# Squared-ReLU attention and a max-out layer on one core: the last part of z loaded by SyncE in f32, cast on ScalarE and VectorE, and transposed earlier

## The chip, the core and the metric

The kernel runs on one core of a Trainium2 chip. The core has four engines that compute here: TensorE (PE; its weight loads are shown as PEld), VectorE (DVE), ScalarE (ACT) and GpSimd (POOL). SyncE (SP) and GpSimd issue DMA transfers. Each engine executes its own instructions in order, and semaphores tie the engines together. The metric is the device time of one execution, in microseconds (us).

## The reference

Eight sequences of 3072 tokens go through an attention without softmax, and its result through a layer that takes the larger of two products.

```
u, v: (8, 3072, 256)    z: (8, 3072, 64)
scores = z @ z.T / 3072
attn = maximum(scores, 0) ** 2
x = (u * (attn @ v)).reshape(24576, 256)
h1, h2 = x @ w1, x @ w2                  # 256 to 1024
out = maximum(h1, h2) @ w_out            # 1024 to 256, f32
```

## The kernel before

**Tiling.** A sequence has 24 blocks of 128 tokens; four blocks make a group, so there are six groups per sequence and 48 steps in all, one for each (sequence b, group s). In a step TensorE forms the scores of the group against the blocks of keys, two blocks at a time (a "pair" k0, 1024 columns in one of three double banks of PSUM). ScalarE or VectorE clamps them at zero into bf16 (`relu`, L281) and squares them (`square`, L287). TensorE multiplies the squares with v into two accumulators (`acc`). The scores are symmetric, so blocks that are needed again are transposed by SyncE's DMA instead of being computed twice. The first steps multiply with v directly; later ones use sums and differences of blocks (`es`) and of v (`lf`, "folds"), which VectorE forms, to save products. Behind a step its result is multiplied by u and goes through the second layer, and SyncE stores it.

**Who orders the work.** TensorE's order is a list that is written out (`pe_order`). The orders of ScalarE, VectorE, SyncE's and GpSimd's queues come from a planner that runs while the kernel is built: `find_orders` (L1865) steps through a model of the engines with fixed durations and gives each free engine the job with the earliest due time; `find_dues` derives these times from TensorE's plan. It runs 24 rounds and the plan in which TensorE ends first is kept. The model's time zero is the start of the first planned job of TensorE. What precedes it, the head, is written out by hand, and the planner is only told when it ends: `HEAD_DONE` (L1801) says when the clamp of tile 4 is done, `idle_from` (L1866) when ScalarE and VectorE become free, in nanoseconds.

**The head** is where the change lies. z of the first sequence must reach TensorE as `zT`, transposed and in bf16:

- z's 24 blocks are loaded in three parts. SyncE loads blocks 0 to 4 and 5 to 8 (ZF = 9) as f32 into `zf`, a buffer of the pool `opool` (name o_sb, two buffers). VectorE casts the first part into `z_sb_0` (L184), ScalarE the second (L185). GpSimd loads blocks 9 to 23 in one DMA (L183) that casts to bf16 on its way and writes `z_sb_0` directly. GpSimd's loads of v and u for the first sequence (`early_loads`, L2024) come behind it in its queue.
- TensorE starts with products of a blank tile (`idle`, L2020, result `zeros`), six at first. Then it transposes blocks 0 to 8 (`zT_pe`, L124, results tpz and tpz_b) and VectorE copies them from PSUM into `zT`. One more blank product follows.
- `head_pair(k0, part)` (L2007) issues one part of a pair of the first step: part 0 its scores, part 1 its clamp, part 2 its square. Pairs 0 and 2 are scored; two blank products follow; ScalarE clamps pair 0, VectorE pair 2. The scores of pair 4 use the bank that the clamp of pair 0 frees.
- Then come the 16 transposes of blocks 9 to 24 (tpz_c), in a third double bank; ScalarE squares pair 0, VectorE pair 2; VectorE copies tpz_c to `zT` in two pieces; pair 6 is scored, pair 4 clamped by ScalarE. Here the planned jobs begin, with products of pair 0's squares and v.

The planner counts the buffers of `opool` with zf as the first; two later tiles of clamped scores live in them (`HOMES`, L189).

Of the kernel before, what the change touches and what calls it, by code (L numbers as in the profile page):

```python
# [11 lines left out]
def kernel(  # L12
# [17 lines left out]
    nc = tc.nc  # L30
    fp32 = mybir.dt.float32
# [4 lines left out]
    B, S, D = u.shape  # L36
    dqk = z.shape[-1]
    Dff = moe_w1.shape[-1]

    P = 128  # L40
    NSB = S // P
    G = 4
# [31 lines left out]
    opool = ctx.enter_context(tc.tile_pool(name="opool", bufs=2))  # L74
# [4 lines left out]
    pin = tc.keep_in_program_order  # L79
# [22 lines left out]
    def sp_dma(**kw):  # L102
        pin(nc.sync.dma_start(**kw))


    def load(timed=False, **kw):
        dma = pin(nc.gpsimd.dma_start(**kw))  # L107
        if timed:
            tc.add_manual_dep(
                dma.ins,  # L110
                newest[0].name,
                mybir.DependencyInfo(mybir.DependencyClass.Sync, mybir.DependencyReason.DATA),
                reason="timed load",
            )
# [9 lines left out]
    def zT_pe(zT, z_sb, s0, n, tpz=None):  # L124
        flat = z_sb.rearrange("p t d -> p (t d)")
        if tpz is None:
            tpz = mm_psum.tile([P, 8, P], bf16, name="tpz", tag="w0")
        for j in range(n):
            pin(nc.tensor.transpose(tpz[:, j, :], flat[:, ds((s0 + j) * dqk, P)], ident))  # L129
        return lambda copy: pin(copy(zT[:, ds(s0, n), :], tpz[:, :n, :]))  # L130
# [33 lines left out]
    ZF = 9  # L164
# [3 lines left out]
    z_in = z[0].rearrange("(p t) d -> p t d", p=P)  # L168
    for t, n in ((0, 5), (5, ZF - 5)):
        sp_dma(out=zf[:, ds(t, n), :], in_=z_in[:, ds(t, n), :])  # L170
    ident = consts.tile([P, P], bf16)
    make_identity(nc, ident)
    def v_make(tag, name="v_sb"):
# [2 lines left out]
    def z_make(tag):  # L176
        flat = v_make(tag, "z_sb").rearrange("p i g d -> p (i g d)")
        return flat[:, : (NSB + 2) * dqk].rearrange("p (t d) -> p t d", d=dqk)

    z_sb_0 = z_make("v12")  # L180
    pin(nc.gpsimd.memset(z_sb_0[:, 0:1, :], 0.0))
    pin(nc.gpsimd.memset(z_sb_0[:, NSB + 1 : NSB + 2, :], 0.0))
    load(out=z_sb_0[:, 1 + ZF : 1 + NSB, :], in_=z_in[:, ZF:, :])  # L183
    pin(nc.vector.tensor_copy(z_sb_0[:, 1:6, :], zf[:, :5, :]))  # L184
    pin(nc.scalar.copy(z_sb_0[:, 6 : 1 + ZF, :], zf[:, 5:ZF, :]))  # L185
    q.zT = zpool.tile([P, NSB + 1, P], bf16, name="zT")
# [81 lines left out]
    def score(q, out_ps, j, k, s, q0, n):  # L268
        half = ds(j * dqk, dqk)
        matmul(  # L270
            out_ps,
            q.zT[half, k + 1 - j, :],
            q.zT[half, ds(G * s + 1 - j + q0, n), :],
            start=True,
            stop=True,
        )
# [4 lines left out]
    def relu(eng, out_ap, in_ap):  # L281
        if eng == "ACT":
            pin(nc.scalar.activation(out_ap, in_ap, AF.Relu))  # L283
        else:
            pin(nc.vector.tensor_single_scalar(out=out_ap, in_=in_ap, scalar=0.0, op=ALU.max))
# [7 lines left out]
    def copy(eng, out_ap, in_ap):  # L293
        pin(nc.scalar.copy(out_ap, in_ap) if eng == "ACT" else nc.vector.tensor_copy(out_ap, in_ap))  # L294
# [122 lines left out]
    def s_tile(key):  # L417
        return tile_of("mm", key)

    def by_tokens(s_ps):  # L420
        return s_ps.rearrange("p m (t x) -> p m t x", t=2)
# [1010 lines left out]
    for name in "s20 a10 s21 b10 a11 a12 b11 a13 s22 b12 b13 s23 a00 a01 s10 b00 b01 s11 a02 a03 b02 b03 s12 o00 s13 o01 o02 o03".split():  # L1432
        n, i = last - int(name[1]), int(name[2])
# [37 lines left out]
    begins, t = [], 0  # L1471
# [326 lines left out]
    for key, before in zip(pe_order, [None] + pe_order):  # L1798
        if key[0] == "score" and (before is None or plain_modes.get(before) == "F"):
            jobs[key].ways = {"PE": jobs[key].ways["PE"] + 2 * SWITCH}  # L1800
    HEAD_DONE = {("relu", 0, 4): 900}  # L1801
    HEAD_JOBS = HEAD | {("relu", 0, k0) for k0 in (0, 2, 4)} | {("square", 0, k0) for k0 in (0, 2)}


# [31 lines left out]
    plan, t = {}, 0  # L1836
# [26 lines left out]


    def find_orders():  # L1865
        idle_from = {"PE": 0, "ACT": 900, "DVE": 1300, "SP": 0, "POOL": 0}  # L1866
        ready = {e: [] for e in idle_from}
        emitted = []
        dma_free = [10000]

        def release(j):
            at = 0
            for d in j.all_deps:
                at = max(at, d.done)
            for d in j.all_after:
                at = max(at, d.begin + 1)
            for e in j.ways:
                ready[e].append((at, j))

        def settle(j, begin, ns):  # L1880
            j.begin, j.done = begin, begin + ns + j.lag
            if j.key in FIRST_LOADS:
                j.done = FIRST_LOADS[j.key]
            elif j.dma:

                dma_free[0] = max(dma_free[0], begin + DMA_START["SP" if "SP" in j.ways else "POOL"]) + (DMA_FULL if begin < DMA_FULL_TO else DMA_PART) * j.dma
                j.done = dma_free[0] + (DMA_LATE if begin > 125000 and j.key[0] != "zT" else DMA_END)
                if "SP" in j.ways:
                    idle_from["SP"] = max(begin + SP_ISSUE, dma_free[0] - DMA_AHEAD)
            for nxt, _ in j.succ:  # L1890
                nxt.waits -= 1
                if not nxt.waits:
                    release(nxt)

        for j in list(jobs.values()):
            if not j.waits and j.key not in HEAD_JOBS:
                release(j)
        for key in [k for k in jobs if k in HEAD_JOBS]:
            settle(jobs[key], HEAD_DONE.get(key, -1), 0)
            for e in jobs[key].ways:  # L1900
                ready[e] = [r for r in ready[e] if r[1] is not jobs[key]]


        def left_to_act(j, t):
            if j.key[0] not in ("relu", "g", "oc") or "ACT" not in j.ways:
                return False
            return max(t, idle_from["ACT"]) + j.ways["ACT"] <= max(t, idle_from["DVE"]) + j.ways["DVE"] + RELU_BIAS


        def left_to_dve(j, t):  # L1910
            if j.key[0] != "square":
                return False
            return max(t, idle_from["DVE"]) + j.ways["DVE"] <= max(t, idle_from["ACT"]) + j.ways["ACT"] + SQUARE_BIAS

        while len(emitted) < len(jobs) - len(HEAD_JOBS):
            best = None
            for e, todo in ready.items():
                if e == "DVE":
                    todo = [r for r in todo if not left_to_act(r[1], r[0])]
                if e == "ACT":  # L1920
                    todo = [r for r in todo if not left_to_dve(r[1], r[0])]
                if not todo:
                    continue
                found = [(max(t, idle_from[e]), j.due, j) for t, j in todo]
                at, _, j = min(found, key=lambda x: x[:2])

                if e != "PE":
                    near = [x for x in found if x[0] <= at + PATIENCE]
                    at, _, j = min(near, key=lambda x: x[1] + WAIT_COST * (x[0] - at))
                if best is None or at < best[0]:  # L1930
                    best = at, e, j
            assert best, [k for k, j in jobs.items() if j.begin is None][:20]
            at, e, j = best
            for o in j.ways:
                ready[o] = [r for r in ready[o] if r[1] is not j]
            idle_from[e] = at + (j.ways[e] if e != "POOL" else 1000)
            settle(j, at, j.ways[e])
            emitted.append((j, e))
        return emitted
# [63 lines left out]
    def take(pool, key):  # L2003
        b = bufs[pool, key]
        b.tile = b.make() if b.slot is None else b.make(f"w{b.slot}")

    def head_pair(k0, part):  # L2007
        key = (0, k0)
        if part == 0:
            take("mm", key)  # L2010
            for j in range(2):
                score(q, s_tile(key)[:, j, :], j, k0 + j, 0, 0, G)
        elif part == 1:
            if k0 % G == 0:
                take("A", (0, k0 // G))
            relu("DVE" if k0 == 2 else "ACT", a_rows(steps[0], k0), by_tokens(s_tile(key)))
        else:
            square("ACT" if k0 == 0 else "DVE", a_half(a_tile(steps[0], k0 // G), k0))

    def idle(n):  # L2020
        for _ in range(n):
            matmul(zeros, blank[:, :P], blank, start=True, stop=True)
# [4 lines left out]
            take(*use)  # L2027
        jobs[key].fn("POOL")
    zeros = acc_psum.tile([P, GW], fp32, name="zeros", tag="acc0")
    idle(6)  # L2030
    tpz = [
        acc_psum.tile([P, 8, P], bf16, name="tpz", tag="acc1"),
        mm_psum.tile([P, 2, 8, P], bf16, name="tpz_b", tag="w0")[:, 0],
# [1 line left out]
    two = [zT_pe(q.zT, z_sb_0, 0, 5, tpz[0]), zT_pe(q.zT, z_sb_0, 5, ZF - 5, tpz[1])]  # L2035
    for part in two:
        part(nc.vector.tensor_copy)
    idle(1)
    head_pair(0, 0)
    head_pair(2, 0)  # L2040
    idle(2)
    head_pair(0, 1)
    head_pair(2, 1)
    head_pair(4, 0)
    tpz = mm_psum.tile([P, 2, 8, P], bf16, name="tpz_c", tag="w0")
    two = [zT_pe(q.zT, z_sb_0, ZF + 8 * i, 8, tpz[:, i]) for i in range(2)]
    head_pair(0, 2)
    head_pair(2, 2)
    for part in two:
# [41 lines left out]
```

## Time and profile before

| | |
|---|---|
| median of 3 runs | 885.77 us (884.52 to 887.27) |
| the profiled execution | 885.35 us, of which the profile's span is 883.5 us |
| granted clock of TensorE (mean, from the clock's record) | 1.00 |
| TensorE, VectorE, ScalarE, GpSimd busy | 877.1, 804.7, 753.3, 105.5 us |
| DMA traffic | 146.18 MB, mean 165 GB/s |

How to read the lines of the profile: in a timeline a row gives start and duration in us, the engine, the line of the kernel, the operation, the tile written and the tile read, shapes, and how many instructions are merged into the row (x16). In brackets stands the idle time of the engine ahead of it and what ended it. "SPq" and "POOL DMA_DIRECT2D" rows are the issuing of a DMA, not its transfer. "issue" is time in which an engine waited for nothing that the profile shows. L86 is the helper through which all matrix products go, so products are told apart by their tiles: `zeros` are the blank products, `tpz` the transposes, `s_ps` the scores, `acc` the products with v. A line of stretches gives the stretch, its length, the busy time of PE, PEld, DVE, ACT and POOL with their instructions, the granted clock, the DMA engines' share and GB/s. A line of DMA issues gives tiles, queue, operation and count, KB each (as written), and us from the issue to the landing.

### The profile page before, as it was taken

How to read it: one execution, taken by the hardware profiler on the slowest of the kernel's cores; microseconds unless marked ns; L12 is line 12 of the kernel's file. 1: busy time of each engine (PE TensorE's matmuls, PEld its weight loads, DVE VectorE, ACT ScalarE, POOL GpSimd, SP SyncE). 2: the span in 40 equal slices, each digit the busy share in tenths (PEclk: the TensorE clock that was granted, in tenths of full speed). 3: DMA queues.
4: the chain of work that ended last, by engine and by line, in shares of the span. 5: the costliest groups of instructions: out<-in, count | busy, mean ns of one | idle time of the engine just before them, and what ended most of it. 6: DMA issues, size and time to landing. Idle time of an engine off the chain costs nothing.

```text
span 883.5 us, 37928 instructions
## 1 busy us (share of the span) xinstructions
PE 877.1 (99%) x16592; PEld 722.3 (82%) x16592; DVE 804.7 (91%) x1722; ACT 753.3 (85%) x950; POOL 105.5 (12%) x218
## 2 busy tenths in 40 slices
PE   9999999999999999999999999999999999999998
PEld 4468888888888888888877887788778888889886
DVE  6877799999999999999999999999999999999985
ACT  8967998899978999789997899979999799987634
POOL 3101110111001110011100111001110111000000
PEclk9999999999999999999999999999999999999999
DMA  9999999998999999999999999999999998997621
GB/s 167 168 192 195 172 164 202 186 179 147 187 186 154 184 144 177 200 173 154 153 185 171 193 151 164 177 191 168 153 176 172 199 150 155 184 161 124 115 74 73
DMA packets 382454, 146.18 MB, mean 165 GB/s; under 512 B 360656, under 2 KB 362576, under 8 KB 382288
## 3 DMA queue, kind: packets, MB, share of 16 engines
q1 hardware_dynamic: 364272, 114.01, 77.1%
q0 software_dynamic: 18016, 29.75, 24.4%
q8 instruction: 129, 2.11, 1.0%
q14 instruction: 37, 0.30, 0.1%
HBM read 59.77 MB, written 25.17 MB: 96 GB/s over the span
## 4 chain that ended last, share of the span: by engine, by line
PE 97%; DMA 1%; DVE 1%; ACT 1%; issue 0%; DVEq 0%; ACTq 0%
PE acc L86 50%; PE s_ps L86 47%; DMA v_sb<-in_v_dram 1%; PE zeros L86 0%; ACT g_sb L283 0%; DVE gs L300 0%; ACT a_sb L283 0%; ACT w2T_sb L294 0%; PE tpz_c L129 0%; PE w2t_ps L1678 0%; DVE o_sb L297 0%; ACT o_sb L294 0%; DVE w2T_sb L294 0%; DVE o_sb L300 0%; DVE zT L130 0%
## 5 line engine op out<-in xcount | busy, mean ns | idle before, releaser
L86 PEld LDWEIGHTS <-v_sb 64*128 64x128 bf16 x4552 | 328.3, 94 | 65.6 <-issue 3.7
L283 ACT ACTIVATE a_sb<-s_ps 128x1024 bf16<-128x1024 f32 (+1 forms) x334 | 302.5, 941 | 30.2 <-PE s_ps L86 27.0
L86 PEld LDWEIGHTS <-lf 64*128 64x128 bf16 x3240 | 260.4, 94 | 19.4 <-POOLq L94 3.3
L86 PE MATMUL acc<-es,v_sb 64*128 64x256 bf16 x2160 | 274.9, 269 | 0.0
L86 PE MATMUL acc<-es,lf 64*128 64x256 bf16 x1080 | 245.1, 269 | 0.0
L86 PE MATMUL acc<-a_sb,lf 64*128 64x256 bf16 x1224 | 230.0, 269 | 0.0
L86 PE MATMUL s_ps<-xT,w_sb 64*128 64x512 bf16 (+1 forms) x1504 | 210.9, 376 | 0.1
L289 ACT ACTIVATE a_sb<-a_sb 128x1024 bf16<-128x1024 bf16 (+1 forms) x224 | 206.8, 952 | 1.5
L283 ACT ACTIVATE g_sb<-s_ps 128x1024 bf16<-128x1024 f32 x187 | 185.8, 1022 | 18.5 <-PE s_ps L86 16.3
L86 PE MATMUL acc<-aT,lf 64*128 64x256 bf16 x936 | 175.9, 269 | 0.0
L86 PE MATMUL acc<-a_sb,v_sb 64*128 64x256 bf16 (+2 forms) x1424 | 139.3, 284 | 0.8 <-DVE e L297 0.8
L86 PE MATMUL s_ps<-zT 64*128 64x512 bf16 (+2 forms) x774 | 118.2, 333 | 0.5 <-ACT a_sb L283 0.4
L86 PEld LDWEIGHTS <-gs 64*128 64x128 bf16 x2816 | 100.5, 94 | 11.3 <-issue 1.2
L297 DVE TENSOR_TENSOR es<-aT 128x1536 bf16<-128x1536 bf16 (+1 forms) x117 | 106.0, 929 | 0.6
L107 POOL DMA_DIRECT2D u_sb<-in_u_dram x92 | 47.6, 517 | 442.1 <-PE acc L86 270.2
L86 PEld LDWEIGHTS <-w_sb 64*128 64x128 bf16 (+1 forms) x1520 | 75.0, 94 | 27.4 <-POOLq L94 1.5
L86 PEld LDWEIGHTS <-g_sb 64*128 64x128 bf16 x2304 | 86.4, 94 | 11.0 <-POOLq L94 7.4
L300 DVE TENSOR_TENSOR es<-a_sb 128x512 bf16<-128x512 bf16 x198 | 78.1, 417 | 14.2 <-PE acc L86 14.1
L291 DVE TENSOR_TENSOR a_sb<-a_sb 128x1024 bf16<-128x1024 bf16 (+1 forms) x112 | 74.2, 668 | 17.8 <-ACT a_sb L283 17.6
L86 PE MATMUL acc<-aT,v_sb 64*128 64x256 bf16 x936 | 85.5, 269 | 0.0
L86 PE MATMUL s_ps<-wf_sb,gs 64*128 64x128 bf16 x2112 | 84.3, 216 | 0.2 <-issue 0.2
L107 POOL DMA_DIRECT2D v_sb<-in_v_dram x89 | 46.1, 520 | 243.5 <-PE acc L86 129.8
(94 smaller groups left out, 1188.1 us busy)
## 6 DMA issues: line engine op xcount, KB each, us to landing
out_dram<-o_sb SPq DMA_DIRECT2D x47, 512.0 KB, 4.3
u_sb<-in_u_dram POOLq DMA_DIRECT2D x88, 128.0 KB, 4.2
v_sb<-in_v_dram POOLq DMA_DIRECT2D x82, 128.0 KB, 4.0
aT<-a_sb SPq DMA_TRANSPOSE x228, 4.8
z_sb<-in_z_dram POOLq DMA_DIRECT2D x12, 192.0 KB, 4.2
v_sb<-in_v_dram POOLq DMA_DIRECT2D x7, 256.0 KB, 7.1
u_sb<-in_u_dram POOLq DMA_DIRECT2D x4, 256.0 KB, 7.3
w_sb<-in_moe_w_dram POOLq DMA_DIRECT2D x2, 512.0 KB, 9.4
```

The lines of the kernel that those rows point to most:

```text
L86: newest[0] = pin(nc.tensor.matmul(*args, **kw)).ins
L107: dma = pin(nc.gpsimd.dma_start(**kw))
L283: pin(nc.scalar.activation(out_ap, in_ap, AF.Relu))
L289: pin(nc.scalar.activation(ap, ap, AF.Square))
L291: pin(nc.vector.tensor_mul(ap, ap, ap))
L297: pin(nc.vector.tensor_add(*args))
L300: pin(nc.vector.tensor_sub(*args))
```

## The change

The third load of z moves from GpSimd's queue to SyncE's, as its third DMA. It loads f32 into a new tile `zl`, the second buffer of `opool`. ScalarE casts its first eight blocks into `z_sb_0`, VectorE the other seven; both casts are issued behind VectorE's copies of the first nine transposed blocks and ahead of the scores. The 16 transposes of these blocks are issued ahead of the scores of pair 4 instead of behind them. The first run of blank products has five instead of six, and the two blank products behind the scores of pair 2 are gone. The planner is told that ScalarE and the clamp of pair 4 are ready at 1000 instead of 900 ns, and VectorE at 1450 instead of 1300.

```
     for t, n in ((0, 5), (5, ZF - 5)):
         sp_dma(out=zf[:, ds(t, n), :], in_=z_in[:, ds(t, n), :])
+    zl = opool.tile([P, G, D], fp32, name="o_sb").rearrange("p t (n d) -> p (t n) d", d=dqk)
+    sp_dma(out=zl[:, : NSB - ZF, :], in_=z_in[:, ZF:, :])
...
-    load(out=z_sb_0[:, 1 + ZF : 1 + NSB, :], in_=z_in[:, ZF:, :])
...
-    HEAD_DONE = {("relu", 0, 4): 900}
+    HEAD_DONE = {("relu", 0, 4): 1000}
...
-        idle_from = {"PE": 0, "ACT": 900, "DVE": 1300, "SP": 0, "POOL": 0}
+        idle_from = {"PE": 0, "ACT": 1000, "DVE": 1450, "SP": 0, "POOL": 0}
...
-    idle(6)
+    idle(5)
...
     for part in two:
         part(nc.vector.tensor_copy)
+    pin(nc.scalar.copy(z_sb_0[:, 1 + ZF : 9 + ZF, :], zl[:, :8, :]))
+    pin(nc.vector.tensor_copy(z_sb_0[:, 9 + ZF : 1 + NSB, :], zl[:, 8 : NSB - ZF, :]))
     idle(1)
     head_pair(0, 0)
     head_pair(2, 0)
-    idle(2)
     head_pair(0, 1)
     head_pair(2, 1)
-    head_pair(4, 0)
     tpz = mm_psum.tile([P, 2, 8, P], bf16, name="tpz_c", tag="w0")
     two = [zT_pe(q.zT, z_sb_0, ZF + 8 * i, 8, tpz[:, i]) for i in range(2)]
+    head_pair(4, 0)
     head_pair(0, 2)
     head_pair(2, 2)
```

More of the change, by code (lines that the diff above doesn't have):

```diff
@@ L170 @@
         sp_dma(out=zf[:, ds(t, n), :], in_=z_in[:, ds(t, n), :])
+    zl = opool.tile([P, G, D], fp32, name="o_sb").rearrange("p t (n d) -> p (t n) d", d=dqk)
+    sp_dma(out=zl[:, : NSB - ZF, :], in_=z_in[:, ZF:, :])
     ident = consts.tile([P, P], bf16)
@@ L182 @@
     pin(nc.gpsimd.memset(z_sb_0[:, NSB + 1 : NSB + 2, :], 0.0))
-    load(out=z_sb_0[:, 1 + ZF : 1 + NSB, :], in_=z_in[:, ZF:, :])
     pin(nc.vector.tensor_copy(z_sb_0[:, 1:6, :], zf[:, :5, :]))
@@ L1800 @@
             jobs[key].ways = {"PE": jobs[key].ways["PE"] + 2 * SWITCH}
-    HEAD_DONE = {("relu", 0, 4): 900}
+    HEAD_DONE = {("relu", 0, 4): 1000}
     HEAD_JOBS = HEAD | {("relu", 0, k0) for k0 in (0, 2, 4)} | {("square", 0, k0) for k0 in (0, 2)}
@@ L1865, in find_orders @@
     def find_orders():
-        idle_from = {"PE": 0, "ACT": 900, "DVE": 1300, "SP": 0, "POOL": 0}
+        idle_from = {"PE": 0, "ACT": 1000, "DVE": 1450, "SP": 0, "POOL": 0}
         ready = {e: [] for e in idle_from}
@@ L2029 @@
     zeros = acc_psum.tile([P, GW], fp32, name="zeros", tag="acc0")
-    idle(6)
+    idle(5)
     tpz = [
@@ L2037 @@
         part(nc.vector.tensor_copy)
+    pin(nc.scalar.copy(z_sb_0[:, 1 + ZF : 9 + ZF, :], zl[:, :8, :]))
+    pin(nc.vector.tensor_copy(z_sb_0[:, 9 + ZF : 1 + NSB, :], zl[:, 8 : NSB - ZF, :]))
     idle(1)
@@ L2040 @@
     head_pair(2, 0)
-    idle(2)
     head_pair(0, 1)
     head_pair(2, 1)
-    head_pair(4, 0)
     tpz = mm_psum.tile([P, 2, 8, P], bf16, name="tpz_c", tag="w0")
     two = [zT_pe(q.zT, z_sb_0, ZF + 8 * i, 8, tpz[:, i]) for i in range(2)]
+    head_pair(4, 0)
     head_pair(0, 2)
```

## The prediction

> **What bounds the kernel now.** I read the page first: busy times, then the chain that ended last.
>
> ```profile
> span 883.5 us, 37928 instructions
> PE 877.1 (99%) x16592; PEld 722.3 (82%) x16592; DVE 804.7 (91%) x1722; ACT 753.3 (85%) x950; POOL 105.5 (12%) x218
> PE 97%; DMA 1%; DVE 1%; ACT 1%; issue 0%; DVEq 0%; ACTq 0%
> ```
>
> TensorE is busy for 877.1 of 883.5 us and holds 97% of the chain. Busy is not the same as unhindered, so the next view gives busy time by stage (length of the stretch first, then each engine).
>
> ```profile
> 0.00:9.00 9.00, 7.30 (x52) 3.37 (x52) 4.48 (x8) 5.29 (x6) 5.26 (x16) 1.00 0.84 151
> 9.00:112.00 103.00, 102.90 (x1295) 69.97 (x1293) 81.63 (x165) 85.50 (x103) 13.40 (x26) 1.00 1.18 179
> 112.00:115.00 3.00, 2.21 (x46) 1.71 (x42) 2.33 (x7) 2.63 (x4) 0.32 (x3) 1.00 1.13 183
> 115.00:860.00 745.00, 744.75 (x14830) 631.86 (x14826) 703.71 (x1520) 649.67 (x823) 86.52 (x176) 1.00 1.03 167
> ```
>
> From 9 us on TensorE idles 0.10 us, then 0.79 us around 113 us, then 0.25 us in 745 us. The edit removes no product there, so what it does by design happens in the first 9 us. There the timeline decides (start, duration, engine, work).
>
> ```profile
> 0.74 0.86 SPq L103 DMA_DIRECT2D o_sb<-in_z_dram  x2
> 1.19 2.74 PE L86 MATMUL zeros<-blank 128*128 128x512 bf16 x6 [1.19 <-DVE blank L166]
> 1.49 0.67 POOL L107 DMA_DIRECT2D z_sb<-in_z_dram  x1
> 3.04 0.35 DVE L184 CAST z_sb<-o_sb 128x320 bf16<-128x320 f32 x1 [1.90 <-DMA o_sb<-in_z_dram]
> 3.40 0.41 ACT L185 CAST z_sb<-o_sb 128x256 bf16<-128x256 f32 x1 [1.37 <-DMA o_sb<-in_z_dram]
> 3.73 0.63 PE L129 MATMUL tpz<-ident,z_sb 128*128 128x128 bf16 x5
> 4.19 0.39 PE L129 MATMUL tpz_b<-ident,z_sb 128*128 128x128 bf16 x4
> 4.39 0.49 DVE L130 COPY zT<-tpz 128x640 bf16<-128x640 bf16 x1 [1.00 <-PE tpz L129]
> 4.80 0.41 DVE L130 COPY zT<-tpz_b 128x512 bf16<-128x512 bf16 x1
> 4.94 0.61 PE L86 MATMUL s_ps<-zT 64*128 64x512 bf16 x4
> 5.37 1.02 ACT L283 ACTIVATE a_sb<-s_ps 128x1024 bf16<-128x1024 f32 x1 [1.57 <-PE s_ps L86]
> 5.48 0.60 PE L86 MATMUL zeros<-blank 128*128 128x512 bf16 x2
> 5.59 1.22 DVE L285 TENSOR_SCALAR a_sb<-s_ps 128x1024 bf16<-128x1024 f32 x1 [0.38 <-PE s_ps L86]
> 6.43 1.06 ACT L289 ACTIVATE a_sb<-a_sb 128x1024 bf16<-128x1024 bf16 x1
> 6.45 0.39 PE L86 MATMUL s_ps<-zT 64*128 64x512 bf16 x2 [0.36 <-ACT a_sb L283]
> 6.77 1.07 PE L129 MATMUL tpz_c<-ident,z_sb 128*128 128x128 bf16 x16
> 6.84 0.69 DVE L291 TENSOR_TENSOR a_sb<-a_sb 128x1024 bf16<-128x1024 bf16 x1
> 7.39 5.71 ACT L283 ACTIVATE a_sb<-s_ps 128x1024 bf16<-128x1024 f32 x6
> 7.77 0.39 PE L86 MATMUL s_ps<-zT 64*128 64x512 bf16 x2
> 7.88 1.29 DVE L130 COPY zT<-tpz_c 128x1024 bf16<-128x1024 bf16 x2 [0.34 <-PE tpz_c L129]
> 8.00 1.03 PE L86 MATMUL acc<-a_sb,v_sb 64*128 64x512 bf16 x8
> 9.22 0.10 PEld L86 LDWEIGHTS <-zT 64*128 64x128 bf16 x2 [0.47 <-DVE zT L130]
> ```
>
> The reader should see a chain of hand-overs: z lands, is cast, transposed, copied (zT), scored (4.94), clamped by ScalarE (5.37) and only then frees the bank for the scores of tile 4 (6.45). TensorE fills the gap before 6.45 with two blanks and idles 0.36 us; only afterwards do the 16 transposes run, and the first products start at 8.00. The score of tile 10 waits again, at 9.22, for the second copy of those transposes.
>
> **One blank fewer.** The six blanks start 0.42 us apart ((2.74 - 0.63) / 5, taking the last one's length as that of the five transposes' row), yet dropping one doesn't buy 0.42. The casts end at 3.39 and 3.81, so the first transposes can start at about 3.5 instead of 3.73, and at the early half-rate they take 0.107 each, a quarter of a blank's 0.42, not the 0.092 of now ((4.19 - 3.73) / 5). The last of five then starts at 3.97 and the copy at about 4.3 instead of 4.39. I take a gain of 0.1 us for the copy, the scores (4.84) and ScalarE's first clamp (5.27); bounds 0 and 0.23.
>
> **The third load on SyncE.** SyncE issues its two loads in 0.86 us, so the third costs it 0.43 us and ends at about 2.0; its next instruction comes after 12 us, nothing is queued behind. GpSimd loses one issue of 0.67 us, so the v loads start that much earlier: both streams now run together. When does the third land? The issue view gives size and time to landing:
>
> ```profile
> z_sb<-in_z_dram POOLq DMA_DIRECT2D x1, 240.0 KB, 4.3
> o_sb<-in_z_dram SPq DMA_DIRECT2D x1, 160.0 KB, 2.3
> o_sb<-in_z_dram SPq DMA_DIRECT2D x1, 128.0 KB, 2.2
> ```
>
> The first two land at 0.74 + 2.3 = 3.04 and 0.74 + 0.43 + 2.2 = 3.37: 128 KB in 0.33 us. The third is 480 KB (15 x 64 x 4 bytes x 128 rows), so 1.25 us if it has the queues alone: 4.6. If the v loads take every second turn it needs 2.5 us: 5.9, beside 5.8 now. I take 4.9, near the early end, because GpSimd's stream ramps up slowly, as the two stretches here show (GB/s last):
>
> ```profile
> 2.00:3.00 1.00, 1.00 (x4) 0.42 (x3) 0.00 (x0) 0.02 (x1) 1.00 (x3) 1.00 0.82 267
> 3.00:4.00 1.00, 1.00 (x6) 0.40 (x5) 0.35 (x1) 0.41 (x1) 1.00 (x3) 1.00 0.94 86
> ```
>
> While SyncE's loads ran, 267 GB/s moved; with GpSimd's alone, 86 between 3 and 4 us. SyncE's third load should find room there.
>
> **The two new casts.** ScalarE: 256 columns took 0.41 and a 1024-wide operation 1.02, so 512 columns take 0.41 + 256 x 0.61 / 768 = 0.61. VectorE: 0.35 x 448 / 320 = 0.49. Both engines run in order. Behind ScalarE's cast stand the clamp of tile 0, its square and all clamps to 13 us; behind VectorE's stand the clamp of tile 2, its square and the copies of zT. Landing at 4.9, ScalarE casts 4.94 to 5.55 and the clamp moves from 5.37 to 5.57: 0.20 late. VectorE is free at 5.21 - 0.1 = 5.11, casts to 5.60 and clamps at 5.62, 0.03 late. If the load lands at 4.6, ScalarE's cast ends at 5.25, hidden in the 1.57 us that it waits now, and the clamp is 0.10 early.
>
> **The transposes moved.** The 16 take about 1.0 us and now fit between 5.55 and 6.65, where TensorE had the blanks and 0.36 us of idling while ScalarE's clamp runs (5.57 to 6.59). Scores of tile 4 follow at 6.65, of tile 6 once VectorE's clamp ends at 6.84. The first products need the square of tile 0: 5.57 + 1.06 + 1.06 = 7.69, so they start at 7.74 instead of 8.00. The copies start right after VectorE's square (6.87 + 0.69 = 7.56) and end at 8.85 instead of 9.17, so tile 10's scores start at 8.90 instead of 9.22: 0.32 gained. The two blanks dropped cost nothing to lose, since the transposes stand in their place; without that cover they'd be 0.43 us.
>
> **What is late next.** ScalarE. Its clamps run without a gap, 0.95 us each, two in 1.90, while TensorE issues two scores and twelve products every 1.73:
>
> ```profile
> 12.99 3.78 ACT L283 ACTIVATE o_sb<-s_ps 128x1024 bf16<-128x1024 f32 x4
> 14.20 0.59 PE L86 MATMUL s_ps<-zT 64*128 64x512 bf16 x4
> ```
>
> With three score buffers the second score of the 14.20 group (14.42) needs the clamp that ends at 12.99 + 0.95 = 13.94: 0.48 in hand, about 0.43 after the hand-over. TensorE 0.32 early and ScalarE 0.20 late use up 0.52, so TensorE waits 0.1 there. Net: 0.32 - 0.1 = 0.2 us gained. At 4.6: 9.22 becomes 8.86, ScalarE is early too, gain 0.36. At 5.9: clamp at 6.57 (1.20 late), VectorE's cast to 6.43, copies to 9.67, tile 10 at 9.72 (0.50 late), and 1.20 - 0.50 - 0.43 = 0.27 more at 14.4: a loss of 0.8. The third load's buffer is the second of the o_sb pair; its next writer comes at 12.99, long after the casts, at no cost.
>
> **The planner's constants.** Two start times of ScalarE and VectorE (900 to 1000, 1300 to 1450) feed the ordering of those two engines and of the DMA queues; TensorE's own order is fixed. So all of them may be dealt anew, at a cost the trace can't show. What a new order can gain is bounded: TensorE's idle time behind the head, 0.10 + 0.79 + 0.25 = 1.1 us. What it can lose has one example:
>
> ```profile
> 112.73 0.42 DVE L297 TENSOR_TENSOR lf<-v_sb 128x512 bf16<-128x512 bf16 x1 [0.64 <-DMA v_sb<-in_v_dram]
> 113.99 0.39 PE L86 MATMUL acc<-a_sb,v_sb 64*128 64x256 bf16 x4 [0.79 <-DVE e L297]
> ```
>
> I take 0 for it, with -1.1 and +3.2 (four such waits of 0.8) for the range.
>
> **Sum.** The profiled execution took 885.35 us (span 883.5 plus 1.85 around it); less 0.2 gives 885.15. The runs' median, 885.77, lies 0.42 above that execution, so as a median I forecast 885.77 - 0.2, rounded to 885.5.
>
> **Rivals.** *The load lands late.* The v loads share the same engines from 2.8 us on and the third load, at half rate, lands at 5.9. For it: now GpSimd's z load, ahead of v, needs until 5.8. Against it: the 86 GB/s. It gives +0.8: 886.5. The Trainium skill, "DMA: Bandwidth & Descriptors", section "Queues, rings and completion order", says that each DMA engine takes turns between the queues that have work; by that rule the half rate holds and this rival is right. The trace of before, where the two streams hardly overlap, can't show it.
>
> *The clock stays low.* TensorE's early blanks start 0.42 us apart, the two at 5.48 take 0.60 in all, and the transposes of part one already come faster than 0.107: the rate doubles near 4.1 us. If the pause between five blanks and the transposes puts that off until the head is through, at 7.5 us, part one's copy is hardly later, but scores take 0.43 instead of 0.22 and the 16 transposes 1.7: clamps 5.62 and 6.02, tile 10 about 9.35, 0.13 late: 885.9. Against it: the pause is under 0.2 us. The skill's "TensorE: Matmul & The Clock Gate", section "What's actually happening", says that the rate follows a free-running activity window of about 3.4 us, not a count of products; by it one blank matters only through that pause.
>
> *The new order makes waits.* The place is a join like 113 us: a fold of v, queued on VectorE ahead of the subtractions of e, waits for its load, and TensorE waits 0.8 us for what stands behind. VectorE is busy 91% and executes in order, and every one of the eight sequences loads and folds its v, so an order that is dealt wrongly can repeat this wait in each. From four of them (3.2 - 0.2 = 3.0) it shows as slower: about 889. Against it: in 745 us only 0.25 us of idling remains now.
>
> *The new order removes the wait at 113 us and the rest:* -0.2 - 1.1, 884.5.
>
> **How the numbers follow.** Chances: forecast 0.47, late load 0.17, low clock 0.06, new waits 0.24, waits removed 0.06. A measurement of this kernel tells 0.3%, 2.7 us, from no change. Only the new waits leave that band by themselves: slower 0.24. Faster would need 2.7 us, over twice the 1.3 that head and idle time hold, so 0.07 for what I have overlooked and for scatter (the runs of before reach from 884.52 to 887.27). Same 0.69. The range goes from 883.3 (waits removed, less the 1.2 by which the lowest run lies under the median) to 889.0 (new waits); the forecast's own is 884.3 to 886.6.
>
> **What would show it.** Right: the third z load lands between 4.6 and 5.2; ScalarE's cast 0.6 us long, right before its first clamp at 5.3 to 5.7; transposes ended by 6.7; first products at 7.5 to 7.8; tile 10's scores at 8.9; TensorE's idle time behind 9 us again near 1.1. Wrong: a cast ending after 6 us, zeros or transposes at half-rate after 5 us, or idle rows of TensorE of 0.5 us and more behind 20 us that are not there now.

## The result and the profile after

The changed kernel takes 889.65 us (median of 6 runs, 888.44 to 890.85), the kernel before 884.67 (6 runs, 884.42 to 887.27): a ratio of 1.005 with a 95% interval of 1.0037 to 1.0063. It is 5.0 us slower, beyond the range's upper end of 889.0. The profiled execution took 889.39 us.

From the page of the changed kernel, the span, the busy times and the chain that ended last:

```profile
span 887.6 us, 37924 instructions
PE 878.9 (99%) x16589; PEld 752.0 (85%) x16589; DVE 805.0 (91%) x1723; ACT 753.1 (85%) x951; POOL 105.0 (12%) x217
...
PE 97%; DMA 1%; issue 1%; DVE 1%; ACT 0%; SPq 0%; POOL 0%; POOLq 0%; ACTq 0%
PE acc L86 50%; PE s_ps L86 46%; DMA o_sb<-in_z_dram 1%; ACT g_sb L284 0%; PE tpz_c L129 0%; DVE gs L301 0%; ACT w2T_sb L295 0%; PE w2t_ps L1679 0%; SPq L103 0%; DVE e L298 0%; DVE e L301 0%; DVE o_sb L298 0%; ACT o_sb L295 0%; DVE w2T_sb L295 0%; DVE o_sb L301 0%
```

These shares hardly move. One new name tells it: a load of z (o_sb<-in_z_dram) now stands on the chain. The busy times by stretch, with the columns as before:

```profile
0.00:9.00 9.00, 4.83 (x19) 1.69 (x19) 1.48 (x5) 1.72 (x3) 4.73 (x15) 1.00 0.78 171
9.00:112.00 103.00, 102.26 (x1218) 68.08 (x1218) 80.84 (x162) 84.71 (x102) 12.24 (x22) 1.00 1.15 175
112.00:115.00 3.00, 3.00 (x52) 2.72 (x50) 2.34 (x5) 3.00 (x4) 0.52 (x1) 1.00 1.47 164
115.00:860.00 745.00, 744.68 (x14854) 660.30 (x14851) 706.32 (x1527) 652.41 (x827) 87.48 (x179) 1.00 1.04 167
```

In the first 9 us TensorE was busy for 7.30 us before and for 4.83 us now. From 9 us on it idles 0.74 us to 112 us (0.64 of it is the rest of the same wait) and 0.32 us in the long stretch; the wait of 0.79 us at 113 us doesn't occur in this execution. The timeline of the head names the wait:

```profile
0.74 1.34 SPq L103 DMA_DIRECT2D o_sb<-in_z_dram  x3
1.19 2.31 PE L86 MATMUL zeros<-blank 128*128 128x512 bf16 x5 [1.19 <-DVE blank L166]
3.53 0.69 PE L129 MATMUL tpz<-ident,z_sb 128*128 128x128 bf16 x5
4.26 0.49 DVE L130 COPY zT<-tpz 128x640 bf16<-128x640 bf16 x1 [0.88 <-PE tpz L129]
5.01 1.04 PE L86 MATMUL s_ps<-zT 64*128 64x512 bf16 x4
8.97 0.62 ACT L2039 CAST z_sb<-o_sb 128x512 bf16<-128x512 f32 x1 [5.17 <-DMA o_sb<-in_z_dram]
8.97 0.40 DVE L2040 CAST z_sb<-o_sb 128x448 bf16<-128x448 f32 x1 [3.86 <-DMA o_sb<-in_z_dram]
9.49 1.02 ACT L284 ACTIVATE a_sb<-s_ps 128x1024 bf16<-128x1024 f32 x1
9.64 1.89 PE L129 MATMUL tpz_c<-ident,z_sb 128*128 128x128 bf16 x16 [3.60 <-ACT z_sb L2039]
12.29 1.85 PE L86 MATMUL acc<-a_sb,v_sb 64*128 64x512 bf16 x8
19.16 0.59 PE L86 MATMUL s_ps<-zT 64*128 64x512 bf16 x4
```

Both casts wait until 8.97 for the third load. TensorE idles 3.60 us, then the 16 transposes take 1.89 us instead of 1.07 and eight products 1.85 instead of 1.03: TensorE runs at half its rate, up to 13.97. (PEclk shows 1.00 there, since the clock's record of this execution begins with its first change, at 13.95 us.) The first products start 12.29 - 8.00 = 4.29 us late, and the scores that were issued at 14.20 come at 19.16, 4.96 late. Less the 0.79 us at 113 us this is 4.2; the span grew by 4.1. The issue view has the load itself:

```profile
o_sb<-in_z_dram SPq DMA_DIRECT2D x1, 480.0 KB, 7.3
o_sb<-in_z_dram SPq DMA_DIRECT2D x1, 160.0 KB, 2.3
o_sb<-in_z_dram SPq DMA_DIRECT2D x1, 128.0 KB, 2.2
```

Issued at 1.66, it lands 7.3 us later, at 8.95, not at 4.9. Counting in both traces the packets that start in each microsecond shows what it competes with (z: the 128 rows of the third part, of which 4 and 6 start before 3 us; v: rows of the v loads):

```
us          3-4  4-5  5-6  6-7  7-8  8-9
before   z   44   77    3    0    0    0    (GpSimd's queue, ahead of v)
         v    0   19   91   95   96   97
after    z   26   41   36   10    7    2    (SyncE's queue, beside v)
         v    7   35   55   84   91   96
```

The two queues take turns about evenly from 4 to 6 us. What then remains of z, 19 rows, needs three more microseconds, in which v gets 271.

The single packets show what the last rows wait for. Each of these loads ends with 16 packets of 4 bytes in its queue, as many as there are DMA engines by the profile's page. Of this load's 16, eight start before 6 us, six more before 7, and the last two at 8.28 and 8.65. The rows of z that start after 7 us form two series with steps of 0.31 us (7.03, 7.34, 7.66, 7.97 and 7.09, 7.40, 7.71, 8.02, 8.34); a row of z takes 0.16 us and one of v about 0.17, so one row of v fits between two of z. This reads as two engines that had fallen behind and still took turns evenly, while the other fourteen had only v left. The trace doesn't name a packet's engine, so that is a reading, and it doesn't say why the two were behind.

### The profile page after: what moved, and what is told of

Read it like the earlier page. It is cut to its first block, busy times and chain, and to the rows that moved or that the text cites. A ratio compares the mean times of both kernels' runs of the same rounds, so it can differ in the third digit from the quotient of the medians.

```text
span 887.6 us, 37924 instructions
## 1 busy us (share of the span) xinstructions
PE 878.9 (99%) x16589; PEld 752.0 (85%) x16589; DVE 805.0 (91%) x1723; ACT 753.1 (85%) x951; POOL 105.0 (12%) x217
## 4 chain that ended last, share of the span: by engine, by line
PE 97%; DMA 1%; issue 1%; DVE 1%; ACT 0%; SPq 0%; POOL 0%; POOLq 0%; ACTq 0%
PE acc L86 50%; PE s_ps L86 46%; DMA o_sb<-in_z_dram 1%; ACT g_sb L284 0%; PE tpz_c L129 0%; DVE gs L301 0%; ACT w2T_sb L295 0%; PE w2t_ps L1679 0%; SPq L103 0%; DVE e L298 0%; DVE e L301 0%; DVE o_sb L298 0%; ACT o_sb L295 0%; DVE w2T_sb L295 0%; DVE o_sb L301 0%
## 5 line engine op out<-in xcount | busy, mean ns | idle before, releaser
L86 PEld LDWEIGHTS <-v_sb 64*128 64x128 bf16 x4552 | 339.4, 94 | 53.2 <-issue 4.1
L86 PEld LDWEIGHTS <-lf 64*128 64x128 bf16 x3240 | 268.5, 94 | 11.8 <-POOLq L94 3.2
L86 PE MATMUL acc<-a_sb,lf 64*128 64x256 bf16 x1224 | 234.5, 269 | 0.0
L86 PE MATMUL s_ps<-xT,w_sb 64*128 64x512 bf16 (+1 forms) x1504 | 215.1, 376 | 0.3 <-POOLq L94 0.2
L86 PE MATMUL acc<-aT,lf 64*128 64x256 bf16 x936 | 179.3, 269 | 0.0
L86 PE MATMUL acc<-a_sb,v_sb 64*128 64x256 bf16 (+2 forms) x1424 | 142.6, 286 | 0.1
L86 PE MATMUL s_ps<-zT 64*128 64x512 bf16 (+2 forms) x774 | 122.8, 335 | 0.0
L86 PEld LDWEIGHTS <-gs 64*128 64x128 bf16 x2816 | 104.1, 94 | 9.0 <-issue 0.6
L86 PEld LDWEIGHTS <-w_sb 64*128 64x128 bf16 (+1 forms) x1520 | 82.4, 94 | 24.1 <-POOLq L94 2.1
L86 PEld LDWEIGHTS <-g_sb 64*128 64x128 bf16 x2304 | 88.9, 94 | 9.9 <-POOLq L94 7.3
```

Source lines behind the costliest of these rows:

```text
L86: newest[0] = pin(nc.tensor.matmul(*args, **kw)).ins
```

## The experiments

Theory 1 is what this profile suggests: the third load is starved beside the v loads, TensorE waits for it, and its idle time keeps its clock low. The rivals blame the planner's constants, the blanks, the casts, or SyncE's load by itself. Ratios are to the kernel before, which was run beside them (median 884.69 us for experiments 1 to 4, 884.95 for 5 to 8), with their 95% intervals. "Below the change" compares with the 889.65 us above.

**1. GpSimd's load back, all else of the change kept.**

```
-    zl = opool.tile([P, G, D], fp32, name="o_sb").rearrange("p t (n d) -> p (t n) d", d=dqk)
-    sp_dma(out=zl[:, : NSB - ZF, :], in_=z_in[:, ZF:, :])
+    load(out=z_sb_0[:, 1 + ZF : 1 + NSB, :], in_=z_in[:, ZF:, :])
...
-    pin(nc.scalar.copy(z_sb_0[:, 1 + ZF : 9 + ZF, :], zl[:, :8, :]))
-    pin(nc.vector.tensor_copy(z_sb_0[:, 9 + ZF : 1 + NSB, :], zl[:, 8 : NSB - ZF, :]))
```

> The change with GpSimd's casting load of z's third part put back ahead of the v loads, and no third load and no casts on SyncE, ScalarE and VectorE; the moved transposes, the dropped blanks and the planner's constants stay. Theory 1 (the third load is starved beside the v loads, TensorE waits for it and its clock stays low): the load lands at 5.8 us as before, the transposes run from about 5.9 to 6.9, the clock rises near 4.1 us, the first products start at 7.4 to 7.8, and the time is 0.3 to 1.5 us below that of before. Rival (the dropped blanks or the planner's constants cost the time): it stays 4 to 5 us above that of before.

Measured: 884.10 us against 884.69 for the kernel before, ratio 0.9985 (0.9971 to 0.9999). In its timeline the transposes stand in TensorE's wait for the clamp of pair 0, as the change intends:

```profile
5.41 1.02 ACT L283 ACTIVATE a_sb<-s_ps 128x1024 bf16<-128x1024 f32 x1 [1.62 <-PE s_ps L86]
6.00 1.07 PE L129 MATMUL tpz_c<-ident,z_sb 128*128 128x128 bf16 x16 [0.42 <-DMA z_sb<-in_z_dram]
7.00 0.61 PE L86 MATMUL s_ps<-zT 64*128 64x512 bf16 x4
7.57 1.04 PE L86 MATMUL acc<-a_sb,v_sb 64*128 64x512 bf16 x8
...
112.73 0.42 DVE L297 TENSOR_TENSOR lf<-v_sb 128x512 bf16<-128x512 bf16 x1 [1.36 <-DMA v_sb<-in_v_dram]
114.33 0.40 PE L86 MATMUL acc<-a_sb,v_sb 64*128 64x256 bf16 x4 [1.51 <-DVE e L297]
```

The first products start 0.43 us earlier than before; the loss is gone. The last two rows show where such a gain can go again: v's load lands as late as it did, at 112.7, and the wait at 113 us has grown from 0.79 to 1.51 us in this execution.

**2. The planner's constants alone.**

```
-    HEAD_DONE = {("relu", 0, 4): 900}
+    HEAD_DONE = {("relu", 0, 4): 1000}
-        idle_from = {"PE": 0, "ACT": 900, "DVE": 1300, "SP": 0, "POOL": 0}
+        idle_from = {"PE": 0, "ACT": 1000, "DVE": 1450, "SP": 0, "POOL": 0}
```

> The kernel of before with the planner's new constants alone (1000, 1000, 1450). The built order differs in two neighbouring VectorE instructions only (a fold and a subtraction of e near 113 us). Theory 1: within 1 us of before, and the wait of 0.79 us at 113 us changes. Rival (the constants cost the time): 4 to 5 us above before.

Measured: 884.57 us, ratio 0.9998 (0.9981 to 1.0016). The constants swap two neighbours of VectorE and cost nothing that can be measured. In this execution the fold found its load landed and TensorE's wait was not there, but after experiment 1, which has the same swap and the wait, it can't be credited to the swap.

**3. The wait kept warm.** TensorE's wait is filled with blanks.

```
     head_pair(2, 1)
+    idle(17)
     tpz = mm_psum.tile([P, 2, 8, P], bf16, name="tpz_c", tag="w0")
```

> The change with 17 blank products more, in TensorE's wait ahead of the 16 transposes. It separates the wait from the low clock. Theory 1: the third load still lands at about 9 us, but the clock rises near 4.1 us; transposes take 1.0 instead of 1.9 us, the first products start at about 11.6 instead of 12.29 and run at the full rate: 1.3 to 2.0 us below the change, 2.5 to 3.5 above before. Rival (the blanks dropped are all of it, the late load is harmless): within 0.5 us of before. Rival (the clock has no part): equal to the change within 0.5 us.

Measured: 888.72 us, ratio 1.0041 (1.0029 to 1.0054): 0.9 us below the change, less than expected.

```profile
5.41 3.84 PE L86 MATMUL zeros<-blank 128*128 128x512 bf16 x17
8.86 0.62 ACT L2039 CAST z_sb<-o_sb 128x512 bf16<-128x512 f32 x1 [4.82 <-DMA o_sb<-in_z_dram]
9.53 1.07 PE L129 MATMUL tpz_c<-ident,z_sb 128*128 128x128 bf16 x16 [0.28 <-ACT z_sb L2039]
11.54 1.04 PE L86 MATMUL acc<-a_sb,v_sb 64*128 64x512 bf16 x8 [0.40 <-ACT a_sb L290]
```

The load is as late, but transposes and products run at the full rate again, and what then holds the first products is ScalarE's square. So the wait itself is about 4.0 of the 5.0 us, the low clock the other 0.9; since the two ratios' intervals overlap, the split is rough. (The two profiled executions lie 1.47 us apart, 889.39 and 887.92.)

**4. v held back.** GpSimd waits for the fourth blank product ahead of its loads of v and u.

```
-    for key in early_loads:
-        for use in news(jobs[key]):
-            take(*use)
-        jobs[key].fn("POOL")
     zeros = acc_psum.tile([P, GW], fp32, name="zeros", tag="acc0")
-    idle(5)
+    idle(4)
+    mark()
+    for key in early_loads:
+        for use in news(jobs[key]):
+            take(*use)
+        jobs[key].fn("POOL")
+    idle(1)
```

> The change with a wait on GpSimd ahead of its loads of v and u, for the fourth blank product, so that they are issued from about 3.1 us on instead of 1.5. Theory 1: the third load has the queues alone, lands between 4.5 and 5.0 us, transposes are through by 6.8, the clock rises near 4.1 us, v's first part lands before 7 us, and the time is 0.3 to 1.5 us below before. Rival (SyncE's f32 load and the casts are slow by themselves): the load lands after 6 us as well and the time stays 2 us or more above before.

Measured: 886.66 us, ratio 1.0024 (1.0009 to 1.004). Both theories missed. Three views of it: the issues, the stretches from 3 to 7 us (GB/s last) and the timeline.

```profile
o_sb<-in_z_dram SPq DMA_DIRECT2D x1, 480.0 KB, 4.0
```
```profile
3.00:4.00 1.00, 0.92 (x7) 0.44 (x6) 0.33 (x1) 0.40 (x1) 0.61 (x1) 1.00 0.49 108
4.00:5.00 1.00, 0.85 (x10) 0.50 (x10) 0.68 (x2) 0.00 (x0) 1.00 (x3) 1.00 1.06 348
5.00:6.00 1.00, 0.47 (x4) 0.00 (x0) 0.46 (x3) 0.32 (x1) 1.00 (x3) 1.00 0.49 56
6.00:7.00 1.00, 0.65 (x12) 0.65 (x13) 1.00 (x2) 1.00 (x2) 1.00 (x3) 1.00 0.68 86
```
```profile
6.35 1.07 PE L129 MATMUL tpz_c<-ident,z_sb 128*128 128x128 bf16 x16 [0.88 <-ACT z_sb L2041]
10.05 1.04 PE L86 MATMUL acc<-a_sb,v_sb 64*128 64x512 bf16 x8 [2.09 <-DMA v_sb<-in_v_dram]
```

With hardly a v packet beside it (3 before 5 us), the load lands at 1.66 + 4.0 = 5.7 us. That is 3.3 earlier than in the change, so the v loads cause most of the delay. But it is 1.1 later than the 4.6 that I had for a load alone: SyncE's third load, too, starts slowly, at 108 GB/s from 3 to 4 us. The v loads, issued from 3.39 us on, start slowly in turn (14 rows from 5 to 6 us, where the 56 GB/s hold the last 7 rows of z as well, then 86 GB/s), and TensorE waits 2.09 us for v. The profiled execution, 888.44 us, is one of four in ten (888.42 to 889.84) whose mean granted clock is 0.998; in its trace the clock is halved from 10.98 to 14.39 us, after that wait. The other six, at 0.999 or 1.00, took 884.98 to 887.03.

**5. The same f32 load from GpSimd's queue, ahead of v.**

```
-    sp_dma(out=zl[:, : NSB - ZF, :], in_=z_in[:, ZF:, :])
+    load(out=zl[:, : NSB - ZF, :], in_=z_in[:, ZF:, :])
```

> The change with its third load, still f32 into zl and cast by ScalarE and VectorE, issued by GpSimd ahead of the v loads instead of by SyncE. Theory 1 (what makes the load late is that the v loads run beside it from another queue): behind one another in one queue the load lands at 5.6 to 6.2 us, the clamp of pair 0 waits for the cast and starts at 6.3 to 6.8, the first products at 8.2 to 8.8, and the time is 0 to 1.5 us above before, at least 3 below the change. Rival (f32 into a buffer and two casts are the cost, whatever the queue): within 1 us of the change.

Measured: 885.65 us, ratio 1.0002 (0.9993 to 1.0012). Issue and timeline:

```profile
o_sb<-in_z_dram POOLq DMA_DIRECT2D x1, 480.0 KB, 4.5
```
```profile
1.50 0.69 POOL L107 DMA_DIRECT2D o_sb<-in_z_dram  x1
5.98 0.62 ACT L2039 CAST z_sb<-o_sb 128x512 bf16<-128x512 f32 x1 [2.18 <-DMA o_sb<-in_z_dram]
6.50 1.02 ACT L284 ACTIVATE a_sb<-s_ps 128x1024 bf16<-128x1024 f32 x1
8.66 1.04 PE L86 MATMUL acc<-a_sb,v_sb 64*128 64x512 bf16 x8 [0.40 <-ACT a_sb L290]
```

As theory 1 has it, the same bytes, ahead of v in one queue, land at 6.0, and 4.0 of the 5.0 us are back. So most of what was lost lies in the second queue. But f32 and the casts are not free: against experiment 1, which differs in them alone, the first products start 1.09 us later (8.66 against 7.57) and the median is 1.5 us higher (885.65 against 884.10, from different rounds). That uses up what the moved transposes gain.

**6. The moved transposes and dropped blanks alone**, with the constants of before: experiment 1 with 900, 900 and 1300.

> The moved transposes and the dropped blanks alone: GpSimd's casting load and the planner's constants as before. Theory 1: the first products start at 7.5 to 7.7 us instead of 8.00, the fold near 113 us waits for its load as before and takes back part of it: 0.2 to 0.8 us below before. Rival (the move loses something later): 1 us or more above before.

Measured: 884.57 us, ratio 0.9995 (0.9986 to 1.0005). The first products start at 7.82, later than expected, because this execution's clock rose only at 6.7 us, and the wait at 113 us is 0.7 us. The sign is as expected, but the gain can't be told from none.

**7. The casts behind the clamps and squares of pairs 0 and 2.**

```
         part(nc.vector.tensor_copy)
-    pin(nc.scalar.copy(z_sb_0[:, 1 + ZF : 9 + ZF, :], zl[:, :8, :]))
-    pin(nc.vector.tensor_copy(z_sb_0[:, 9 + ZF : 1 + NSB, :], zl[:, 8 : NSB - ZF, :]))
     idle(1)
...
     head_pair(2, 1)
+    head_pair(0, 2)
+    head_pair(2, 2)
+    pin(nc.scalar.copy(z_sb_0[:, 1 + ZF : 9 + ZF, :], zl[:, :8, :]))
+    pin(nc.vector.tensor_copy(z_sb_0[:, 9 + ZF : 1 + NSB, :], zl[:, 8 : NSB - ZF, :]))
     tpz = mm_psum.tile([P, 2, 8, P], bf16, name="tpz_c", tag="w0")
...
     head_pair(4, 0)
-    head_pair(0, 2)
-    head_pair(2, 2)
```

> The change with the two casts behind the clamps and squares of pairs 0 and 2 in ScalarE's and VectorE's order (and ahead of the transposes, as the data demand). It takes away the queueing behind the casts and leaves the late load. Theory 1: the load still lands at about 9 us; clamps and squares run from 5.4 on, so that only the transposes, at 9.6 to 11.5, and the scores of pair 4 stand between the load and the first products, which start at 11.8 to 12.2 instead of 12.29: at most 1 us below the change. Rival (the queueing of the clamps behind the casts is the main cost): 2.5 us or more below the change.

Measured: 888.6 us (887.29 to 891.06), ratio 1.0042 (1.0029 to 1.0056), 1.0 below the change.

```profile
5.24 1.02 ACT L284 ACTIVATE a_sb<-s_ps 128x1024 bf16<-128x1024 f32 x1 [1.40 <-PE s_ps L86]
7.55 0.62 ACT L2046 CAST z_sb<-o_sb 128x512 bf16<-128x512 f32 x1 [0.20 <-DMA o_sb<-in_z_dram]
8.22 1.89 PE L129 MATMUL tpz_c<-ident,z_sb 128*128 128x128 bf16 x16 [2.81 <-ACT z_sb L2046]
10.87 1.20 PE L86 MATMUL acc<-a_sb,v_sb 64*128 64x512 bf16 x8
```

In the profiled execution, the fastest of them, the load landed at 7.5 instead of 9, so its start isn't comparable as such. The distance is: from cast to first products 3.32 us, as in the change (8.97 to 12.29). Clamps that ran early saved nothing there, since the transposes at half rate and the scores behind them took that time anyway.

**8. The load and the casts alone**, in the kernel of before.

```
+    zl = opool.tile([P, G, D], fp32, name="o_sb").rearrange("p t (n d) -> p (t n) d", d=dqk)
+    sp_dma(out=zl[:, : NSB - ZF, :], in_=z_in[:, ZF:, :])
...
-    load(out=z_sb_0[:, 1 + ZF : 1 + NSB, :], in_=z_in[:, ZF:, :])
...
         part(nc.vector.tensor_copy)
+    pin(nc.scalar.copy(z_sb_0[:, 1 + ZF : 9 + ZF, :], zl[:, :8, :]))
+    pin(nc.vector.tensor_copy(z_sb_0[:, 9 + ZF : 1 + NSB, :], zl[:, 8 : NSB - ZF, :]))
     idle(1)
```

> The kernel of before with the third load on SyncE and the two casts alone; six blanks, two more behind the scores of pair 2, transposes behind the scores of pair 4 and the planner's constants as before. Theory 1: the load lands at 8.5 to 9.1 us, the first clamps wait for the casts until 9.4, the first products start at 12 to 13 us and the time is 4 to 5.5 us above before, as with the whole change. Rival (the load costs this only together with the dropped blanks or the moved transposes): less than 2 us above before.

Measured: 890.88 us, ratio 1.0059 (1.0044 to 1.0074). One part alone has the whole loss, 5.9 us here, slightly more than expected; the first products, at 13.40, are later than the 12 to 13 expected too. Its timeline, and its busy times by stretch, with the granted clock third from the end:

```profile
9.04 0.62 ACT L2039 CAST z_sb<-o_sb 128x512 bf16<-128x512 f32 x1 [5.23 <-DMA o_sb<-in_z_dram]
10.64 0.61 PE L86 MATMUL s_ps<-zT 64*128 64x512 bf16 x2 [4.31 <-ACT a_sb L284]
13.40 1.91 PE L86 MATMUL acc<-a_sb,v_sb 64*128 64x512 bf16 x8
```
```profile
5.00:6.00 1.00, 1.00 (x7) 0.23 (x6) 0.35 (x1) 0.00 (x0) 0.34 (x1) 1.00 0.99 199
6.00:9.00 3.00, 0.33 (x2) 0.09 (x1) 0.00 (x0) 0.00 (x0) 0.00 (x0) 0.91 1.07 204
9.00:11.00 2.00, 0.36 (x2) 0.10 (x1) 1.92 (x3) 1.92 (x3) 0.00 (x0) 0.50 1.08 192
11.00:13.00 2.00, 2.00 (x18) 1.63 (x17) 0.30 (x1) 1.59 (x2) 0.00 (x0) 0.50 1.12 206
```

Here TensorE had been granted the full clock, lost it while it waited, and ran its transposes and first products at 0.50.

## Why the prediction was wrong

**One blank fewer: right for the transposes and the copy,** which start at 3.53 and 4.26, against 3.5 and 4.3. The 0.1 for the first clamp did not come reliably: with five blanks it starts at 5.24, 5.41 and 5.65 where the clock rises at 4.39, 4.88 and 6.67 us (experiments 7, 1 and 6), against 5.37 before, where it rises at 4.10.

**The step that failed is the landing of the third load.** I put it between 4.6 and 5.9 us and took 4.9; it landed at 8.95. Two readings went wrong.

- *The slow stretch from 3 to 4 us.* I read the 86 GB/s as a slow start of GpSimd's stream that leaves room for SyncE. Experiment 4 shows SyncE's own load, alone, at 108 GB/s in the same microsecond and at 348 in the next, and v behind it at 86 or less until 7 us. Nor was 86 as low as it looks: a casting load is counted as written in bf16 (240 KB for the 480 KB of f32), and at full pace such loads reach 195 to 199 (kernel before, 6 to 9 us). These loads began slowly from either queue. So "alone" is 5.7, not 4.6, and in the change 55 of the load's 128 rows had not started at 5 us, while v was coming up to speed.
- *The upper bound.* Half of the rate for all of it gave 5.9. That is an average over all rows, and the casts wait for the last row. Fourteen of the 16 closing packets had started by 7 us; the last two came at 8.28 and 8.65.

The rival "the load lands late" thus named the mechanism, with a price of +0.8 us, about a sixth of what it cost. The Trainium skill's rule of turns ("DMA: Bandwidth & Descriptors", "Queues, rings and completion order") agrees with the even counts from 4 to 6 us, and the steps of 0.31 us after 7 us fit it too. Why the last rows started so late stays open; in experiment 7 the same load landed at 7.5 us.

**What stands behind the landing was priced right.** For a landing at 5.9 us my sum gave a clamp at 6.57 and a loss of 0.8. In experiment 5 the load lands at 5.98, the clamp starts at 6.50, and the median is 0.7 above the kernel before (the ratio's interval reaches from 0.6 us below to 1.1 above). With experiment 3's landing at 8.86, the same sum gives 0.8 + 2.96 = 3.8; that experiment, with the late load at full clock, measures 4.0.

**The casts' lengths: right for ScalarE** (0.62 against 0.61), **too long for VectorE** (0.40 against 0.49). What I said stands behind them did stand behind them, but experiment 7 shows that their order added nothing while TensorE was slow.

**The low clock: a rival that came true together with the late load, not instead of it.** I gave it 0.06 for a pause of under 0.2 us between blanks and transposes. That pause was short, 3.50 to 3.53 us; in the profiled execution the clock had not risen when the wait of 3.60 us behind the scores began, and rose only after it. Experiment 3 prices the low clock at 0.9 us; the wait itself costs 4.0. The change's other five executions have mean granted clocks of 0.996 or 0.998, as experiments 8 and 7 have, whose clock was granted and lost in the wait; that it went the same way there is likely, but they have no trace.

**The transposes moved: right in kind.** With GpSimd's load they fill TensorE's wait and the first products start at 7.57 (experiment 1), inside the 7.5 to 7.8 that I named. The gain in time, 0.6 us at the medians (884.10 against 884.69), has an interval that all but touches none.

**The planner's constants: 0 was right, and the new waits, with a chance of 0.24, did not come.** The chance of "slower" rested on this rival. The order changed in two neighbouring instructions, and experiment 2 measures no difference. The time came out slower, but by another cause than the one that carried the chance.

## What to carry to other kernels

A transfer that moves to a queue of its own doesn't leave the others' way: from 4 to 5 us 89 rows of z started with v held back (experiment 4) and 41 with v beside it. A transfer that was first in line became one of two. Here it paid to keep what the next stage needs first ahead, in the same queue, of what can wait, and its price is read from the landing of its last row. Waits of 2.1 to 4.3 us were followed by a halved clock (experiments 4, 7 and 8); blanks kept the clock up but did not shorten the wait.

The best version that ran is experiment 1: the moved transposes with GpSimd's casting load, 0.9985 of the kernel before.

## What the runs showed of the hardware

The clock's changes stand on a fixed grid. From the traces (us from the span's start, share granted):

```
after           13.95 full
experiment 4     4.15 full   10.98 half   14.39 full
experiment 7     4.39 full    7.81 half   11.22 full
experiment 8     5.05 full    8.47 half   15.29 full
```

Within one execution all distances are 3.41 us or twice that, and the first grant falls anywhere from 4.1 (before) to 6.7 us (experiment 6) with nearly the same blanks ahead of it. "TensorE: Matmul & The Clock Gate" of the Trainium skill ("What's actually happening") has a free-running window of about 3.4 us; these traces agree. In the changed kernel 13.95 less three times 3.41 is 3.7 us: if the grid holds there, the blanks, from 1.19 us on, filled about three quarters of the window that ended then, and it brought no grant. In the kernel before, the 3.41 us ahead of the grant at 4.10 were filled for 2.91, about 85%.
